# One kernel, several small reorderings: conversion steps at fixed places, operands at 128 bytes, a drain of GpSimd before the last expert

## The chip, the cores and the metric

The kernel runs on one core of a Trainium2 chip. The metric is the device time of one execution in microseconds (us). Three timed runs of the kernel before gave 777.03, 773.71 and 778.46 us; their median is 777.03. One further execution was recorded by the hardware profiler, and every row below comes from that one. The engines are TensorE (PE for its matmuls, PEld for the loads of stationary operands that run beside them), VectorE (DVE), ScalarE (ACT), GpSimd (POOL) and SyncE (SP, which only starts transfers).

## The reference, cut to what matters

Attention in chunks of 32 queries, each seeing 16 keys to the left, 8 to the right and 8 memory keys; a mixture of 8 experts in which each token has one expert and each expert exactly 384 tokens, given out greedily in the order of the gate's logits; and a last network with a SoLU (h times its softmax) and a normalisation.

```python
for c in range(nc):                                  # attention, per chunk of 32
    scores = scale * np.matmul(q_c, k_full.transpose(0, 1, 3, 2))
    a = np.exp(scores - max); a = a / (sum + 1e-09)
    out[:, :, c_start:c_end] = np.matmul(a, v_full)
logits = x @ w_gate                                  # x: 3072 x 512
for idx in np.argsort(-logits.flatten()):            # tok, e = idx // 8, idx % 8
    if assigned[tok] >= 0 or counts[e] >= cap: continue   # cap = 384
    assigned[tok] = e; counts[e] += 1
for e in range(8):                                   # w1: 512 x 1024, w2: 1024 x 512
    out[mask] = np.maximum(x[mask] @ w1[e], 0.0) @ w2[e]
h = x @ w_in                                         # 512 x 1024
solu = h * softmax(h)
ln = (solu - mean) / sqrt(var + 1e-06) * g_ln
return ln @ w_out                                    # 1024 x 512
```

## The kernel before, in words

**Attention** (`attention`, one loop of 29 turns over 24 tiles of 128 tokens, software-pipelined). For tile i: `score(i)` is 16 matmuls into a bank of scores and the row maxima `mx` on DVE; `less(i)` subtracts them (DVE, tile `p`); `expo(i)` is the exponential on ACT; `sums(i)` is the row sum `sum`, one small step on it, the reciprocal `rec` (all DVE) and the scaling of `p` by `rec` on GpSimd; `trans(i)` transposes p on PE into `t`, which ACT copies to `pt`; `pv(i)` multiplies with v into `o`; `xtrans` and `gate` make the logits `L`. One turn of the loop holds steps of five neighbouring tiles. The keys `kd`, queries `qt` and values `vd` come by transfers that SP starts some tiles ahead. At the end the attention output goes to memory as `x_dram`.

**Conversion.** The last network's two weight matrices arrive as eight-byte floats. `Fixed` turns chunks of 512 KB of them into pairs of single-precision operands (`in_h`, `in_l` and `out_h`, `out_l`): a transfer `raw`, one step on ACT, four on DVE (`e<-v`, `v<-v,e`, `e<-v`, `e<-raw,e`), and two on GpSimd (`v<-v,in_h`, `in_l<-v,e`). Up to seven chunks of w_in (CHUNKS_A) are worked on during attention.

**Routing** (`Route`). One round for each expert: a search of eight steps, each a chain of a few small PE and DVE instructions (`r<-oh,ge`, `sat`, `base`, `ge`), then the compaction that ends in the index list `idx` (`rhs`, `ohl`, `cc`, and `r<-cc,rep`, from which `idx` is made). A round also gives `iw`, the row list by which the expert's weights are fetched. Round 0 has nothing else to run beside it; the later ones run beside the expert before.

**Experts** (`Experts.run`). For expert r: GpSimd gathers three tiles `xg` of 128 rows of `x_dram` by `idx`; `x_prep` transposes each (PE, `tp`) and splits it into a high and a low half, `xh` (ACT) and `xl` (DVE). Each product of two fp32 matrices is three matmuls, high by high, high by low and low by high. `g12` computes h = x w1, hh and hl, and y += h w2, in nine turns f; `g3` computes the last network's h (three tiles t, 24 matmuls of 512 columns each) with `soft` behind it on ACT, DVE and GpSimd; `trans` and `g4` compute the output tile `o`, scaled on ACT into `ob`, which GpSimd scatters to `out` by `idx`. `first_w`, `split_w` make the weights' halves (`w1h` and `w2h` on ACT, `w1l` and `w2l` on DVE). Expert r's g4 runs one expert later, for the last expert at the very end.

**What sets the order.** The program is written out in order for each engine. `Pace` keeps a model clock for each engine; side work (conversion, routing, `soft`) stands in a list of generators, and each call of `beside` (that is `Pace.tick`) puts in the steps whose turn has come by these clocks. So where a side step lands among an engine's instructions is decided when the program is built. In attention the four DVE steps of a conversion chunk can land at any of the loop's `beside` calls. `route.stage` and `route.hold` say which routing round may run and when.

In the profile every instruction that goes through the clocks carries line 421; line 1295 is the start of the kernel and line 1303 its end. In the changed kernel these are lines 435, 1314 and 1322.

## Time and profile before, and how to read them

| what | before |
|---|---|
| timed runs, median (three runs) | 777.03 us (773.71 to 778.46) |
| the profiled execution, its own time | 779.07 us |
| the profiled execution, span of its instructions | 777.3 us |
| PE busy, of the span | 710.9 us, 91% |
| DVE busy, of the span | 518.1 us, 67% |
| chain that ended last, by engine | PE 54%, issue 17%, DVE 17%, DMA 5%, ACT 3%, POOL 2% |

The span is 1.8 us shorter than the execution's own time. Busy time of an engine is the time in which one of its instructions ran. The chain that ended last is followed back from the last instruction, at each step to whatever released it. The stages, by the clock of the trace: attention from 0 to 118.6 us, routing round 0 to 143.4, the first gather to 152.4, expert 0 (g12 and g3) to 221.1, experts 1 to 7 to 747, and the last three output tiles to 764.8; after that only the last scatter and the end of the program. A rate of the granted TensorE clock of 1.00 is 2.4 GHz, one of 0.50 is 1.2 GHz.

### The profile page before, as it was taken

The numbers are of one execution on the slowest core, as the hardware profiler recorded it, in microseconds if no ns is written. First come the engines' busy times: TensorE is split into PE (matmuls) and PEld (weight loads), VectorE is DVE, ScalarE is ACT, GpSimd is POOL, SyncE is SP. The second block draws the span as 40 slices with busy tenths as digits, with TensorE's granted clock in tenths as the row PEclk, the third lists the DMA queues.
The fourth block names the chain that finished last, engine by engine and source line by source line (L and its number), as shares of the span: only waits on it lengthen the run. The fifth ranks groups of instructions, "written<-read, shape, count | busy, mean of one in ns | idle before, by whom it ended". The sixth has DMA issues, their size and how long they took to land.

```text
span 777.3 us, 14615 instructions
## 1 busy us (share of the span) xinstructions
PE 710.9 (91%) x5771; PEld 613.4 (79%) x5771; DVE 518.1 (67%) x1398; ACT 341.6 (44%) x650; POOL 199.6 (26%) x263
## 2 busy tenths in 40 slices
PE   5888884589989999999999999999999999999993
PEld 3676664578879878988898889888988898899882
DVE  5788946578999977962996399549954842554150
ACT  4566640234384364423732463246324642563170
POOL 4354420532351162023202420232023201400121
PEclk9999995789999999999999999999999999999997
DMA  8999982441360062014201520151015200600100
GB/s 258 323 341 340 326 317 72 157 154 57 99 241 1 28 205 94 1 40 153 106 1 33 186 81 1 52 190 58 1 55 190 68 28 27 230 2 1 40 14 27
DMA packets 30020, 89.35 MB, mean 115 GB/s; under 512 B 4224, under 2 KB 4352, under 8 KB 29952
## 3 DMA queue, kind: packets, MB, share of 16 engines
q0 software_dynamic: 13056, 46.14, 17.4%
q1 hardware_dynamic: 16896, 42.28, 15.9%
q8 instruction: 45, 0.74, 0.4%
q14 instruction: 23, 0.19, 0.1%
HBM read 75.83 MB, written 12.58 MB: 114 GB/s over the span
## 4 chain that ended last, share of the span: by engine, by line
PE 54%; issue 17%; DVE 17%; DMA 5%; ACT 3%; POOL 2%; SPq 0%; POOLq 0%; DVEq 0%
PE h L421 24%; PE o L421 11%; PE y L421 10%; DVE e L421 4%; PE tp L421 3%; PE r L421 2%; DMA xg<-x_dram,idx 2%; DMA vd<-in_vx_dram 2%; DVE p L421 1%; DVE mx L421 1%; DVE v L421 1%; DVE ge L421 1%; DVE sum L421 1%; PE s L421 1%; PE xtp L421 1%
## 5 line engine op out<-in xcount | busy, mean ns | idle before, releaser
L421 PE MATMUL y<-hh,w2h 128*128 128x384 f32 x256 | 92.2, 360 | 4.8 <-DVE e L421 4.8
L421 PE MATMUL y<-hl,w2h 128*128 128x384 f32 x256 | 88.4, 345 | 2.0 <-DVE hl L421 2.0
L421 PE MATMUL y<-hh,w2l 128*128 128x384 f32 x256 | 87.4, 341 | 0.0
L421 POOL DMA_INDIRECT out_dram<-ob,idx x24 | 24.4, 1016 | 230.4 <-ACT ob L421 229.9
L421 POOL DMA_INDIRECT raw<-in_w_dram,iw x64 | 62.0, 968 | 81.6 <-PE r L421 34.8
L421 DVE TENSOR_REDUCE nm<-h 128x1 f32<-128x512 f32 x48 | 33.0, 688 | 70.7 <-PE h L421 70.4
L421 PE MATMUL o<-out_h,lh 128*128 128x512 f32 x192 | 77.4, 403 | 0.0
L421 PE MATMUL h<-in_h,yh 128*128 128x512 f32 x192 | 76.6, 399 | 0.0
L421 PE MATMUL h<-in_l,yh 128*128 128x512 f32 x192 | 76.0, 396 | 0.0
L421 PE MATMUL h<-in_h,yl 128*128 128x512 f32 x192 | 75.7, 394 | 0.0
L421 PE MATMUL o<-out_l,lh 128*128 128x512 f32 x192 | 75.4, 393 | 0.3 <-DVE out_l L421 0.3
L421 PE MATMUL o<-out_h,ll 128*128 128x512 f32 x192 | 75.1, 391 | 0.0
L421 ACT ACTIVATE hh<-h 128x384 fp32r<-128x384 f32 x64 | 31.4, 491 | 84.1 <-PE h L421 73.4
L421 ACT CAST w2h<-raw 128x512 fp32r<-128x512 f32 x64 | 39.4, 619 | 49.1 <-PE y L421 49.1
L421 PE MATMUL h<-xh,w1h 128*128 128x384 f32 x256 | 59.9, 347 | 0.4 <-ACT xh L421 0.4
L421 PE MATMUL h<-xh,w1l 128*128 128x384 f32 x256 | 58.4, 345 | 0.0
L421 PE MATMUL h<-xl,w1h 128*128 128x384 f32 x256 | 57.1, 344 | 1.1 <-DVE xl L421 1.1
L421 PEld LDWEIGHTS y<-hh,w2h 128*128 128x128 f32 x256 | 48.4, 189 | 7.5 <-DVE e L421 6.3
L421 DVE TENSOR_TENSOR xl<-tp,xh 128x512 fp32r<-128x512 f32 x24 | 16.6, 691 | 53.1 <-ACT xh L421 53.1
L421 ACT CAST w1h<-raw 128x512 fp32r<-128x512 f32 x64 | 39.6, 619 | 25.6 <-DVE idx L421 25.1
L421 PEld LDWEIGHTS y<-hl,w2h 128*128 128x128 f32 x256 | 48.6, 190 | 2.6 <-DVE hl L421 2.6
L421 DVE TENSOR_TENSOR w2l<-raw,w2h 128x512 fp32r<-128x512 f32 x64 | 43.7, 686 | 8.9 <-ACT w2h L421 8.9
(195 smaller groups left out, 1602.1 us busy)
## 6 DMA issues: line engine op xcount, KB each, us to landing
vd<-in_vx_dram SPq DMA_DIRECT2D x48, 256.0 KB, 5.7
kd<-in_kx_dram SPq DMA_DIRECT2D x48, 176.0 KB, 4.9
qt<-in_q_dram SPq DMA_DIRECT2D x24, 256.0 KB, 5.5
x_dram<-xs SPq DMA_DIRECT2D x6, 1024.0 KB, 9.7
raw<-in_win_dram SPq DMA_DIRECT2D x8, 512.0 KB, 6.0
raw<-in_wout_dram SPq DMA_DIRECT2D x8, 512.0 KB, 3.6
raw<-in_w_dram,iw POOLq DMA_INDIRECT x64, 5.7
xg<-x_dram,idx POOLq DMA_INDIRECT x24, 3.5
```

What stands on the lines that cost most here:

```text
L421: return fn(*args, **kw)
```

## The change

Seven edits. (1) The routing constants (`consts`) are made at the start, among the clearing of buffers, not spread over the first tiles. (2) The attention loop is put in another order: the sums of tile i-1 come first, then score and less of tile i, then up to about 0.65 us of conversion steps on DVE (`pace.fill("dve", ROOM)`, which goes over the 0.65 by the part of a step), the transposes of tile i-2, up to as much of conversion on ACT, the exponential of tile i, and then pv and xtrans of older tiles; `tick` no longer starts conversion steps on DVE in attention (`barred`). Chunks of w_in worked on in attention go from 7 to 6, and the first is fetched one tile sooner. The last group's gate products come in one piece. (3) A tile `pad` of 64 bytes per partition and a `spacer` of 128 bytes in place of 4 move the buffers behind them: the operands of the experts' matmuls then all start at multiples of 128 bytes in their partition. Before, `in_h`, `in_l` and `ident` do; `xh`, `xl`, `yh`, `yl`, `lh`, `ll`, `out_h` and `out_l` start 64 bytes past one, and `hh`, `hl`, the halves of w1 and w2, and `xg` 96 bytes past one. (4) Routing round 1 may start in the third turn of g12 of expert 0 (n = 4) and not ahead of it, and later rounds' stage is set at n = 2. (5) The dummy matmuls ahead of expert 0 write to another PSUM buffer. (6) The output tile of the very last g4 is scaled half on ACT and half on DVE; `soft` gives way once more ahead of its squaring step on ACT. (7) One `drain` of GpSimd stands behind the scatter of the last tile of expert 6, counted from 0.

```diff
@@ -36,12 +36,13 @@
 NEG = -1.0e30
 EVERY_OUT = 7.0
 SPARE_A = 1.38
-CHUNKS_A = 7
+CHUNKS_A = 6
 SIGNAL = 0.19
 EVERY_A = 8.8
 LATE = 1.5
-FIRST_A = 3
-FIRST_C = 8.0
+FIRST_A = 2
+PAD = 16
+ROOM = 0.65
 SPARE = 1.27
 FIT = 0.62
 FIT_OUT = 0.5
@@ -97,6 +98,8 @@
         clear(KD[1])
         nc.gpsimd.memset(KD[2], 0.0)
         nc.vector.memset(VD[0], 0.0)
+        for _ in consts():
+            pass
         clear(KD[3])
         nc.gpsimd.memset(VD[1], 0.0)
         clear(VD[2])
@@ -108,7 +111,6 @@
                 nc.sync.dma_start(wg, wgx)
             if i >= 4:
                 load_v(i - 4)
-        pace.add(consts(), FIRST_C, 0)
         P, PT, XT, mx = {}, {}, {}, {}
 
         def score(i):
@@ -219,21 +221,23 @@
         for i in range(NT + 5):
             if i == NT - 2:
                 pace.limit = 0
-            if i < NT:
-                s = score(i)
-                less(i, s)
-                load_kq(i + AHEAD)
             n = 0
             for _ in sums(i - 1) if 0 <= i - 1 < NT else ():
                 beside(i, n)
                 n += 1
-            if i >= NT and i - 2 < NT:
+            if i < NT:
+                s = score(i)
+                less(i, s)
+                pace.fill("dve", ROOM)
+                load_kq(i + AHEAD)
+            if 0 <= i - 2 < NT:
                 trans(i - 2)
+            if i < NT:
+                pace.fill("act", ROOM)
+                expo(i)
             beside(i, 3)
             if 0 <= i - 3 < NT:
                 pv(i - 3)
-            if i < NT:
-                expo(i)
             load_v(i + AHEAD - 4)
             if i == NT - 2:
                 for u in range(4):
@@ -246,15 +250,13 @@
                 xtrans(i - 4)
             if 5 <= i <= NT and (i - 5) % 4 == 3:
                 gate((i - 5) // 4)
-            if NT < i < NT + 4:
-                gate(NT // 4 - 1, (i - NT - 1,), 2)
+            if i == NT + 3:
+                gate(NT // 4 - 1, range(3), 2)
             if i == NT + 4:
+                gate_last(NT - 1)
                 gate_t(NT // 4 - 1, 3)
-                gate_last(NT - 1)
             if NT + 1 >= i >= 6 and (i - 6) % 4 == 3:
                 gate_t((i - 6) // 4)
-            if 2 <= i < NT:
-                trans(i - 2)
             beside(i, 4)
 
 
@@ -274,6 +276,7 @@
         self.tiles, self.rings = {}, {}
         self.jobs = []
         self.limit, self.spare, self.fit = 9, SPARE_A, FIT
+        self.barred = "dve"
         self.rush, self.late = RUSH, lambda: False
 
     def tile(self, ap):
@@ -388,12 +391,23 @@
             self.now += 0.1
         self.seen = self.now
         for job in list(self.jobs):
-            if job[2] <= self.limit and job[0] <= self.now and (
+            if job[2] <= self.limit and job[0] <= self.now and job[1] != self.barred and (
                     job[1] is None or self.clk[job[1]] <= (self.now + self.rush if self.late() else
                                                          min(self.now + self.spare, self.soon()))):
                 try:
                     self.until(job, next(job[3]))
                 except StopIteration:
+                    self.jobs.remove(job)
+
+    def fill(self, eng, room):
+
+        end = self.clk[eng] + room
+        for job in list(self.jobs):
+            while job[1] == eng and job[0] <= self.clk[eng] < end - 0.3 and job[2] <= self.limit:
+                try:
+                    self.until(job, next(job[3]))
+                except StopIteration:
+                    job[1] = None
                     self.jobs.remove(job)
 
     def soon(self):
@@ -552,7 +566,8 @@
         self.k = ctx.enter_context(tc.tile_pool(name="r_keep", bufs=1))
         self.w = ctx.enter_context(tc.tile_pool(name="r_work", bufs=1))
         self.idx, self.iw = {}, {}
-        self.held, self.stage, self.making, self.hold = False, 0, True, True
+        self.pad = self.k.tile([128, PAD], F32, name="pad")
+        self.held, self.stage, self.hold = False, 0, True
 
     def consts(self, ident):
 
@@ -608,7 +623,6 @@
             yield "spare", "dve"
             setattr(self, name, k.tile([128, n], F32, name=name))
             V.memset(getattr(self, name), value)
-        self.making = False
 
     def open_psum(self, ctx):
         self.ps = ctx.enter_context(self.tc.tile_pool(name="r_ps", bufs=1, space=PSUM))
@@ -870,7 +884,7 @@
         self.yl = k.tile([128, 4, CAP], F32R, name="yl")
         self.lh = k.tile([128, 8, CAP], F32R, name="lh")
         self.ll = k.tile([128, 8, CAP], F32R, name="ll")
-        self.spacer = k.tile([1, 1], F32, name="spacer")
+        self.spacer = k.tile([1, 32], F32, name="spacer")
         self.idx, self.iw = route.idx, route.iw
         self.W, self.C, self.Kc, self.XG, self.WS = {}, {}, {}, {}, {}
         self.scat = []
@@ -1068,6 +1082,7 @@
             self.done.add(("c", r, t, i))
         self.C[r, t] = e
         yield e
+        yield "spare", "act"
         junk = self.wk.tile([128, DM], F32, tag="ob", name="junk", bufs=2)
         A.activation(junk.bitcast(BF), e, AF.Square, accum_out=sq[:, t:t + 1])
         yield "act"
@@ -1127,14 +1142,19 @@
                 between()
         self.need("k", r, t)
         ob = self.wk.tile([128, DM], F32, tag="ob", name="ob", bufs=2)
-        nc.scalar.activation(ob, o, AF.Copy, scale=self.Kc[r][2][:, t:t + 1])
-        nc.gpsimd.memset(self.spacer, 0.0)
+        k, half = self.Kc[r][2][:, t:t + 1], DM // 2 if (r, t) == (E - 1, TT - 1) else DM
+        nc.scalar.activation(ob[:, 0:half], o[:, 0:half], AF.Copy, scale=k)
+        if half < DM:
+            nc.vector.tensor_scalar(ob[:, half:], o[:, half:], k, None, op0=ALU.mult)
+        nc.gpsimd.memset(self.spacer[:, 0:1], 0.0)
         st = nc.gpsimd.indirect_dma_start(
             out=self.out, out_offset=bass.IndirectOffsetOnAxis(ap=self.idx[r][:, t:t + 1], axis=0),
             in_=ob, in_offset=None)
         for o_ in self.scat:
             self.tc.declare_no_dep(st.ins, o_.ins, reason="every token has one row")
         self.scat.append(st)
+        if (r, t) == (E - 2, TT - 1):
+            self.tc.nc.gpsimd.drain()
 
     def run(self, steps):
 
@@ -1155,7 +1175,7 @@
         self.load_w(0, (1, 2))
         self.fixed.hold = False
         self.split_w(0, 0, (1,), True)
-        p = self.ph.tile([128, 4, 128], F32, tag="h", name="warm")
+        p = self.big.tile([128, 4, 128], F32, tag="big", name="warm")
         warm(nc, p, self.route.ones, 40)
         for t in range(TT):
             self.x_prep(0, t)
@@ -1165,7 +1185,6 @@
             self.split_w(0, f, (2,))
         for t in range(TT):
             self.need("x", 0, t)
-        self.route.hold = False
         self.beside.limit, self.beside.fit = 9, FIT_OUT
         self.beside.add(self.fixed.all(1, self.beside, EVERY_OUT, 0, 8))
         start = self.beside.now
@@ -1175,10 +1194,12 @@
             def extra(n, r=r):
                 if n == 2:
                     self.load_w(r, (3,))
+                    self.route.stage = r
+                if n == 4:
+                    self.route.hold = False
                 if r and n in TRANS_AT:
                     m = TRANS_AT.index(n)
                     self.trans(r - 1, m // 2, m % 2)
-            self.route.stage = r
             self.g12(r, extra)
             if r < 2:
                 self.need("y", r, 3)
@@ -1246,9 +1267,7 @@
         beside.tick()
 
     attention(nc, tc, q, kx, vx, wg, ident, x_dram, L, lambda: route.consts(ident), beside, step)
-    while route.making:
-        beside.tick()
-    beside.limit = 9
+    beside.limit, beside.barred = 9, ""
     route.open_psum(ctx)
     fixed.open_out(ctx)
     experts = Experts(ctx, nc, tc, x_dram, w1, w2, fixed, route, beside, ident, out)
```

On DVE in the attention loop, one chunk's first two conversion steps (`e<-v`, `v<-v,e`) stand before like this, between the sums of one tile and the maximum `mx` of the next:

```order
L421 TENSOR_REDUCE mx<-s 128x8
L421 TENSOR_TENSOR p<-s,mx 128x4x2x64
L421 TENSOR_REDUCE sum<-p 128x8
L421 TENSOR_SCALAR sum<-sum 128x8
L421 RECIPROCAL rec<-sum 128x8
L421 TENSOR_SCALAR e<-v 128x512
L421 TENSOR_SCALAR L<-g 128x32
L421 SCALAR_TENSOR_TENSOR v<-v,e 128x512
L421 MEMSET s 32x8x16
L421 TENSOR_REDUCE mx<-s 128x8
L421 TENSOR_TENSOR p<-s,mx 128x4x2x64
```

and in the changed kernel like this:

```order
L435 TENSOR_REDUCE mx<-s 128x8
L435 TENSOR_TENSOR p<-s,mx 128x4x2x64
L435 TENSOR_SCALAR e<-v 128x512
L435 SCALAR_TENSOR_TENSOR v<-v,e 128x512
L435 TENSOR_SCALAR L<-g 128x32
L435 TENSOR_REDUCE sum<-p 128x8
L435 TENSOR_SCALAR sum<-sum 128x8
L435 RECIPROCAL rec<-sum 128x8
L435 MEMSET s 32x8x16
L435 TENSOR_REDUCE mx<-s 128x8
L435 TENSOR_TENSOR p<-s,mx 128x4x2x64
```

The two steps have moved from behind the row sums, where the next tile's `mx` was queued behind them, to behind the subtraction `p<-s,mx`, where the same tile's row sums are queued behind them.

On PE, where expert 0's g3 (`h<-in_h,yh` and its two companions, 72 matmuls) ends and expert 1's g12 (`h<-xh,w1h`) begins, the three transposes of the gathered rows (`tp<-ident,xg`) stand apart among the matmuls of g3 before. The first of the three stands so (39 of the 72 are ahead of it, and `r<-cc,rep`, the last product of the routing round, is behind the 12th):

```order
L421 MATMUL h_3278<-in_l,yh 128x512
L421 MATMUL h_3278<-in_h,yl 128x512
L421 MATMUL tp<-ident,xg 128x128 x4
L421 MATMUL h_3278<-in_h,yh 128x512
L421 MATMUL h_3278<-in_l,yh 128x512
L421 MATMUL h_3278<-in_h,yl 128x512
```

and in the changed kernel all three stand together behind the 72nd, with `r<-cc,rep` behind the 59th:

```order
L435 MATMUL h_3277<-in_h,yh 128x512
L435 MATMUL h_3277<-in_l,yh 128x512
L435 MATMUL h_3277<-in_h,yl 128x512
L435 MATMUL tp<-ident,xg 128x128 x12
L435 MATMUL h<-xh,w1h 128x384 x4
L435 MATMUL h<-xh,w1l 128x384 x4
```

So 13 matmuls of g3 stand between the last product of the routing round and the first transpose, where 27 stood before, and no matmul is left beside the second and the third.

On DVE, between the copy `cc` that this product reads and the index list `idx` made from it, the changed kernel has three steps of the next expert's weights:

```order
L435 CAST cc<-r 128x12
L435 TENSOR_TENSOR w2l<-raw_3203,w2h 128x512
L435 TENSOR_TENSOR w1l<-raw_3201,w1h 128x512
L435 TENSOR_TENSOR w2l<-raw_3203,w2h 128x512
L435 TENSOR_SCALAR idx_3350<-r 128x3
```

Before, one conversion step `e<-v`, one `e<-raw,e` and one row maximum `nm` stand between the two. The drain has no place in this list, which shows no sequencer instructions; on GpSimd it is followed by the small steps `na`, `nv` of the last expert's `soft`.

## Rows read from the trace of the kernel before

**Rows 1.** Windows: stretch, length, busy PE PEld DVE ACT POOL, PEclk, DMA share, GB/s.
```profile
60.00:80.00 20.00, 16.75 (x396) 13.21 (x392) 17.73 (x37) 12.98 (x25) 9.61 (x9) 1.00 0.96 338
152.40:221.10 68.70, 65.43 (x508) 55.50 (x509) 60.00 (x150) 30.91 (x59) 26.55 (x23) 0.95 0.42 137
300.00:400.00 100.00, 98.86 (x588) 88.22 (x587) 73.39 (x221) 42.73 (x82) 18.86 (x27) 1.00 0.21 72
```

**Rows 2.** Timeline, DVE in attention: start, duration, instruction, [idle before it <-its releaser].
```profile
61.51 0.69 DVE L421 TENSOR_REDUCE mx<-s 128x8 f32<-128x512 f32 x1
...
64.00 0.68 DVE L421 TENSOR_REDUCE mx<-s 128x8 f32<-128x512 f32 x1
...
67.85 0.69 DVE L421 TENSOR_REDUCE mx<-s 128x8 f32<-128x512 f32 x1 [1.11 <-PE s L421]
...
70.30 0.38 DVE L421 TENSOR_SCALAR e<-v 128x512 int32<-128x512 int32 x1
70.71 1.43 DVE L421 SCALAR_TENSOR_TENSOR v<-v,e 128x512 int32<-128x512 int32 x1
...
73.25 0.68 DVE L421 TENSOR_REDUCE mx<-s 128x8 f32<-128x512 f32 x1
```

**Rows 3.** Tiles mx and v on DVE: count, ns min/median/max, first to last start.
```profile
L421 DVE TENSOR_REDUCE mx<-s x10: 640/684/692, 61.5 to 97.4; 128x8 f32<-128x512 f32 x10
...
L421 DVE SCALAR_TENSOR_TENSOR v<-v,e x6: 1411/1423/1434, 34.3 to 92.4; 128x512 int32<-128x512 int32 x6
```

**Rows 4.** Timeline: GpSimd beside a conversion step, and such a step later on.
```profile
70.55 1.04 POOL L421 TENSOR_TENSOR p<-p,rec 128x512 f32<-128x512 f32 x1 [1.70 <-DVE rec L421]
...
203.93 0.68 DVE L421 SCALAR_TENSOR_TENSOR v<-v,e 128x512 int32<-128x512 int32 x1
```

**Rows 5.** Timeline, PE from the first gather into g12 of expert 0.
```profile
151.09 0.66 PE L421 MATMUL tp<-ident,xg 128*128 128x128 f32 x4 [1.12 <-DVE xl L421]
...
152.42 0.97 PE L421 MATMUL h<-xh,w1h 128*128 128x384 f32 x4 [0.40 <-ACT xh L421]
...
158.46 0.44 PE L421 MATMUL y<-hl,w2h 128*128 128x384 f32 x1 [1.43 <-DVE hl L421]
...
174.73 0.16 PE L421 MATMUL r<-some,ones 15*128 15x1 f16 x1 [0.78 <-DVE sat L421]
```

**Rows 6.** Windows of PE alone: stretch, length, busy, PEclk, DMA share, GB/s.
```profile
161.00:167.80 6.80, 6.80 (x49) 0.50 0.31 93
```

**Rows 7.** Timeline, GpSimd's first gather for expert 0.
```profile
143.85 1.40 POOL L421 DMA_INDIRECT xg<-x_dram,idx  x1 [4.18 <-ACT w1h L421]
```

**Rows 8.** Timeline, the second gather: DVE, GpSimd and PE.
```profile
207.29 0.15 DVE L421 TENSOR_SCALAR idx<-r 128x3 int32<-128x3 f32 x1
...
207.71 1.07 POOL L421 DMA_INDIRECT xg<-x_dram,idx  x1 [1.95 <-DVE el L421]
...
212.03 0.66 PE L421 MATMUL tp<-ident,xg 128*128 128x128 f32 x4 [0.33 <-DMA xg<-x_dram,idx]
...
223.74 0.44 PE L421 MATMUL h<-xl,w1h 128*128 128x384 f32 x1 [1.08 <-DVE xl L421]
```

**Rows 9.** Groups by form, PE: count, ns min/median/max, first to last start.
```profile
L421 PE MATMUL o<-out_h,lh x24: 389/389/481, 642.6 to 659.3; 128*128 128x512 f32 x24
...
L421 PE MATMUL h<-in_h,yh x24: 394/394/394, 659.9 to 676.0; 128*128 128x512 f32 x24
```

**Rows 10.** Timeline of GpSimd, and the sequencer instructions of the last line.
```profile
730.36 0.96 POOL L421 DMA_INDIRECT out_dram<-ob,idx  x1 [4.42 <-ACT ob L421]
737.39 0.19 POOL L421 TENSOR_TENSOR na<-s 128x1 f32<-128x1 f32 x1 [6.08 <-ACT e L421]
...
766.32 0.96 POOL L421 DMA_INDIRECT out_dram<-ob,idx  x1 [4.32 <-ACT ob L421]
...
L1303 SPq EVENT_SEMAPHORE  x11: 17/28/28, 769.1 to 777.2; - x11
L1303 POOLq DRAIN  x3: 45/102/10418, 766.1 to 777.0; - x3
```

## The prediction, made before the changed kernel ran

> **What bounds the kernel now.** I read the stretches of the span first, since an average over the span hides that its stages have different limits. From 300 to 400 us PE is busy 98.86 of 100 us at full clock [rows 1], and the table puts it at 91% of the whole span: experts 1 to 7 are a stream of matmuls with no room, and nothing in the change takes matmuls out of it. What a reordering can win lies outside: in attention, in the first two handoffs and g12 of expert 0 (65.43 busy of 68.70 us, clock 0.95), and behind the last matmul.
>
> In attention no engine is full, but three are near it. From 60 to 80 us the DMA engines are busy 0.96 of the time at 338 GB/s, DVE 17.73 and PE 16.75 of 20 us [rows 1]. DVE's timeline shows its turn: from one `mx` to the next 2.49 us without conversion (61.51 to 64.00), and 5.40 us with four conversion steps in between, which fill 70.30 to 73.25 [rows 2]. Over ten starts, 61.5 to 97.4, the turn is 35.9/9 = 3.99 us [rows 3].
>
> **The change, part by part**, against the profiled execution's own 779.07 us.
>
> *Attention.* Before, the next tile's `mx` waits behind the conversion steps, and behind `mx` the whole tile. After, they stand behind `p<-s,mx`, where DVE would wait for the exponential before it can sum. So a turn without conversion is two steps of 0.69, the wait, and the sums; the wait is hidden under a pair of steps when there is one. The second point is `v<-v,e`: six times in attention it took 1411 to 1434 ns [rows 3], beside GpSimd's `p<-p,rec` (70.55, 1.04 us, against 70.71), while the same step took 0.68 us at 203.93 with GpSimd just before its own step [rows 4]. In the new order `mx` and `p<-s,mx`, 1.4 us, stand between `rec` and the conversion, so GpSimd has done with `p`. Six times 0.73 us is 4.4 us. DVE alone would give more: at 3.5 us a turn (2.49 plus some 1.0 for the exposed wait or a pair of steps) the 15 turns from 37 to 97 us would save 7. But transfers are busy 0.96 of that time: at 338 GB/s the stage's loads can give back little more than the 4% in which they idle, 2.4 us in 60, and one chunk less (0.52 MB, 1.6 us at that rate). Both together are 4.0, about what the pairing alone gives. I take **-4.5**, bounds 0 (transfers set it anyhow) and -8 (DVE's own sum). The constants go under the first loads, and cost nothing; without that cover they'd be some 3 us.
>
> The Trainium skill ("SBUF — State Buffer", "SBUF: two separate sides") says that a VectorE instruction with two SBUF inputs and a GpSimd one that reads SBUF take one pair of ports in turn, the loser blocked for the whole instruction. The 1.43 against 0.68 us agree. By it alone, GpSimd's conversion steps (1.28 us) can still hold one up in the new order, and the gain would be nearer 2 us.
>
> *First handoff.* The third transpose waits 1.12 us for `xl` of the first tile [rows 5], because it shares a buffer with the dummy matmuls. With these elsewhere it waits for its gather alone. I take **-0.7**, bounds 0 and -1.1.
>
> *g12 of expert 0.* PE waits 1.43 us for `hl` at 158.46, as DVE works off the routing search first, and 0.78 for `sat` [rows 5]; soon after, from 161.0 to 167.8, it runs at half clock with no idle time [rows 6], which costs 3.4 us. The search now starts in the third turn of g12. The wait for `hl` goes, and I think the slow stretch with it, as it came right behind those waits; waits of the search's own kind come back. I take **-4.8** (1.43 + 3.4), bounds -1.4 and -5.6.
>
> *Second handoff.* The price of that. The last routing product now has only 13 matmuls of g3 behind it, at 16.1/23/3 = 0.233 us each [rows 9], 3.0 us. Then come three weight steps ahead of `idx` on DVE (at 0.6 us, about the 0.68 of the step of this size [rows 4], some 2.0 us with `idx`), 0.42 us to the first gather (207.29 to 207.71 [rows 8]), and from there to the first matmul of g12 what the first handoff took, 143.85 to 152.42, less the 1.12 that is not needed [rows 5, 7], 7.45. That is 9.9, less the 3.0 and an estimated 1.3 for the transposes themselves (0.66 for four [rows 8], overlapping): PE idles 5.6 us. Before, it idled 0.33 and 1.08 [rows 8]. The loss is 4.2. Behind such a gap a stretch at half clock is likely; rows 6 price a long one at 3.4, I take 1.0. Together **+5.2**, bounds +2.7 (the weight steps done early) and +7.6. The same order holds for later experts as before, and nothing is added there.
>
> *Alignment.* Matmuls on in_h, which lies on a 128-byte border already, take 394 ns; those on out_h, 64 bytes off one, 389 [rows 9]. So the traces give no sign that a border helps. I take 0, bounds 0 and -2.9 (576 matmuls of g3 by 5 ns).
>
> *Tail.* Half of the last `ob` on each engine: **-0.3**.
>
> *The drain.* GpSimd's last drain took 10.418 us, from 766.1, so to 776.5, though SP, waiting for the last scatter's data, was released at 769.1; two other drains took 0.045 and 0.102 us [rows 10]. So 7.4 us lie behind all data. Either it is work put off for each of the 112 indirect transfers (64 weights, 24 gathers, 24 scatters), 66 ns each, or a fixed delay after any. If the first, the new drain does it for 109 of them and the last one keeps 3: -7.2. The new one stands behind the scatter of 730.36; GpSimd's next work starts at 737.39 [rows 10], and the first scatter behind it is over 20 us off, so even 10 us there are hidden; without that cover they'd be 3 us on the last `soft`. If the second, 0. Nothing in the trace has a drain in mid-kernel. A drain with little to do is short, and a delay that outlasts the data by 7.4 us looks more like a list being worked off than like one transfer: I take **-7.2**, by a little.
>
> Sum: -4.5 - 0.7 - 4.8 + 5.2 - 0.3 - 7.2 = -12.3 us, that is 766.8 for the profiled execution. The median of the timed runs is 2.0 lower, 777.03, and so the forecast is **764.7**; without the drain, 771.9.
>
> **Rivals.** *The drain's delay is fixed* (against: the 0.045 and 0.102 us; for: both come right behind another drain, so they say little): 771.9.
>
> *Transfers set attention, and the second handoff takes all it can*: 0 for attention, +7.6 for the handoff. With the drain's gain 771.6, without 778.8.
>
> *Slower: the exponential comes late.* ACT's conversion steps now stand ahead of the tile's exponential, and DVE's sums wait for it. If ACT had 0.65 us of them in front of every exponential, with what it copies for other tiles (ACT is busy 12.98 of 20 us [rows 1]), a turn would be 1.4 + 1.6 + 1.1 on DVE plus a step, 4.5 us. Twenty-four turns by 0.5 over the present 3.99 are +12 and the 4.5 are not won: 788.4 without the drain's gain, 781.2 with it. It decides from a turn of 4.2 us on. Against it: only 12 of 24 turns have such a step.
>
> *Matmuls gain from the border.* The Trainium skill ("TensorE: Matmul & The Clock Gate", "Back-to-back issue gap") gives 216 ns as a gap for 512 columns, 17 under the 0.233 here; it doesn't name the address. As a mechanism in rows: if the 20 ns over 512/2.4 GHz that g3 shows were due to the address, and as much as 14 in the other 2112 matmuls of 384 and 512 columns, up to 40 us would go; a third of it gives 751. Against: 394 on the border, 389 off it.
>
> **How the numbers follow.** The drain's gain with the other terms near their values 0.42: 764.7, own range 758 to 770. Fixed delay with the others near theirs 0.34: 771.9, 766 to 779. Exponential late, or all of the second rival without the drain's gain, 0.14: 779 to 788. Border 0.10: 740 to 757. One per cent, about what measurement can tell from no change, is 7.8 us: faster means under 769.3. That is 0.40 of the first case, 0.07 of the second and 0.10 of the last: 0.57. Slower, over 784.8, is the greater part of the late exponential without the drain's gain: 0.09. The rest, 0.34, is within 1%. The range from 755 to 781 leaves out most of the border and the upper half of the slow case, 0.18.
>
> **What would show it.** The last drain on line 1322: under 1 us if put-off work, near 10 if fixed; a second row of some 7 to 10 us near 720. In attention `v<-v,e` at 0.7 us and a `mx` turn of 3.6 to 3.8; a turn over 4.2 with DVE idle for `p<-ACT` is the slow rival. No half clock in expert 0's g12; 5 to 6 us of PE waiting for `xg` and `xh` at the start of expert 1. The matmul of g3 at 394 ns again. The prediction is wrong if the drain's 10.4 us stay, or if the second handoff costs over 10 us.

## The result, and the profile after

Four runs of the changed kernel gave 764.3 to 765.93 us, median 765.27; four of the kernel before 773.71 to 778.46, median 776.16. The ratio is 0.9845, with a 95% interval of 0.981 to 0.988: the changed kernel is faster by 1.2 to 1.9%. The forecast was 764.7 (755 to 781). The medians differ by 10.9 us. The profiled execution took 764.67 us, its span is 762.9, 14.4 less than before; that is more than 10.9, since the profiled execution of the kernel before was 2.9 us above its median. The forecast sum, -12.3, lies between the two; its terms came out otherwise, as the next rows show. They cut the span into four stages: up to the first matmul of g12 of expert 0, from there to that of expert 2, then to the last matmul, and the end.

The windows of the changed kernel (from:to, length, busy us of PE, PEld, DVE, ACT and POOL, granted clock, DMA share, GB/s):

```profile
0.00:138.80 138.80, 105.72 (x2231) 83.39 (x2231) 102.17 (x267) 65.93 (x120) 52.02 (x58) 0.90 0.81 286
138.80:298.40 159.60, 145.72 (x943) 124.65 (x944) 135.13 (x343) 76.09 (x144) 53.61 (x57) 0.95 0.33 110
298.40:756.80 458.40, 458.40 (x2598) 405.58 (x2597) 285.41 (x789) 198.42 (x386) 93.29 (x147) 1.00 0.20 70
756.80:762.90 6.10, 0.43 (x2) 0.01 (x1) 0.48 (x1) 0.47 (x1) 0.96 (x1) 0.93 0.11 43
```

The same four windows of the kernel before:

```profile
0.00:152.40 152.40, 109.14 (x2231) 88.35 (x2231) 107.45 (x273) 68.13 (x122) 54.86 (x61) 0.88 0.77 265
152.40:300.00 147.60, 141.72 (x942) 120.58 (x943) 128.18 (x342) 74.14 (x142) 50.66 (x55) 0.98 0.34 114
300.00:764.80 464.80, 459.71 (x2599) 404.50 (x2597) 282.45 (x785) 198.68 (x386) 93.13 (x147) 1.00 0.20 69
764.80:777.30 12.50, 0.39 (x2) 0.00 (x0) 0.00 (x0) 0.69 (x1) 0.96 (x1) 0.65 0.06 21
```

| stage | before | changed | difference | forecast |
|---|---|---|---|---|
| attention, routing round 0, first gather | 152.4 | 138.8 | -13.6 | -5.2 |
| experts 0 and 1 | 147.6 | 159.6 | +12.0 | +0.4 |
| experts 2 to 7 | 464.8 | 458.4 | -6.4 | 0 |
| behind the last matmul | 12.5 | 6.1 | -6.4 | -7.5 |

So two gains were missed (8.4 and 6.4 us) and one loss was (11.6), and they nearly cancel. PE's busy time is what it was (710.3 for 710.9); all that moved is waiting. In experts 2 to 7 PE now never stands still.

**Attention.** DVE's timeline answers to [rows 2]: a pair of conversion steps stands behind `p<-s,mx`, and from one `mx` to the next there are 3.46 us (5.40 for four steps before, 2.49 for none):

```profile
62.64 0.64 DVE L435 TENSOR_REDUCE mx<-s 128x8 f32<-128x512 f32 x1
63.39 0.69 DVE L435 TENSOR_TENSOR p<-s,mx 128x512 f32<-128x512 f32 x1
63.99 0.42 DVE L435 TENSOR_SCALAR e<-v 128x512 int32<-128x512 int32 x1
64.45 0.69 DVE L435 SCALAR_TENSOR_TENSOR v<-v,e 128x512 int32<-128x512 int32 x1
65.06 0.68 DVE L435 TENSOR_REDUCE sum<-p 128x8 f32<-128x512 f32 x1
...
66.10 0.69 DVE L435 TENSOR_REDUCE mx<-s 128x8 f32<-128x512 f32 x1
```

The groups of tile v (count, ns min/median/max, first to last start), answering to [rows 3], and the window from 60 to 80 us, answering to [rows 1]:

```profile
L435 DVE SCALAR_TENSOR_TENSOR v<-v,e x5: 693/693/693, 41.5 to 87.0; 128x512 int32<-128x512 int32 x5
```

```profile
60.00:80.00 20.00, 19.82 (x454) 15.25 (x449) 17.33 (x37) 13.49 (x26) 10.69 (x10) 1.00 0.99 351
```

The step takes 693 ns where it took 1411 to 1434, transfers run at 0.99 and 351 GB/s for 0.96 and 338, and PE is busy 19.82 of 20 us for 16.75.

**Experts 0 and 1.** PE's timeline at the second gather, answering to [rows 8], and in the first g4, where a wait stands that the kernel before does not have:

```profile
209.86 0.66 PE L435 MATMUL tp<-ident,xg 128*128 128x128 f32 x4 [1.59 <-DMA xg<-x_dram,idx]
211.17 0.66 PE L435 MATMUL tp<-ident,xg 128*128 128x128 f32 x4 [0.64 <-DMA xg<-x_dram,idx]
212.60 1.12 PE L435 MATMUL tp<-ident,xg 128*128 128x128 f32 x4 [0.78 <-DMA xg<-x_dram,idx]
214.39 1.01 PE L435 MATMUL h<-xh,w1h 128*128 128x384 f32 x2 [0.67 <-ACT xh L435]
...
282.68 0.80 PE L435 MATMUL o<-out_h,lh 128*128 128x512 f32 x1 [2.90 <-ACT out_h L435]
```

Four waits in a row, 3.7 us, and matmuls behind both places at half clock: the first `tp` took 0.66 us for four and the third 1.12, the first `o` 0.80 where [rows 9] has 0.39 (the granted clock is 0.66 in the mean over 210:220 us, and over 280:290 too).

**The end.** The drains of GpSimd, by line: 1157 is the new one, 1322 the end of the program (count, ns min/median/max, first to last start); then SP's release by the last scatter's data, and the two halves of the last output tile:

```profile
L1157 POOLq DRAIN  x1: 10168/10168/10168, 722.1 to 722.1; - x1
...
L1322 POOLq DRAIN  x3: 51/102/3117, 758.4 to 762.5; - x3
...
L1322 SPq EVENT_SEMAPHORE  x11: 17/28/28, 761.4 to 762.8; - x11
```

```profile
757.40 0.47 ACT L435 ACTIVATE ob<-o,k 128x256 f32<-128x256 f32 x1 [4.80 <-PE o L435]
...
757.91 0.48 DVE L435 TENSOR_SCALAR ob<-o,k 128x256 f32<-128x256 f32 x1 [8.91 <-ACT ob L435]
```

The last drain is 3.1 us long for 10.4 [rows 10], and ends at 758.4 + 3.1 = 761.5, right behind the landing at 761.4. The new one is 10.2 us long, from 722.1 to 732.3, and GpSimd's next step starts at 732.4, 10.0 us behind the scatter where it was 7.0 [rows 10]: the drain held it for some 3 us, and nobody waited.

### The profile page after: what moved, and what is told of

Read it like the earlier page. It is cut to its first block, busy times and chain, and to the rows that moved or that the text cites. A ratio compares the mean times of both kernels' runs of the same rounds, so it can differ in the third digit from the quotient of the medians.

```text
span 762.9 us, 14656 instructions
## 1 busy us (share of the span) xinstructions
PE 710.3 (93%) x5771; PEld 613.6 (80%) x5771; DVE 523.2 (69%) x1399; ACT 340.9 (45%) x650; POOL 199.9 (26%) x263
## 4 chain that ended last, share of the span: by engine, by line
PE 74%; DVE 16%; issue 4%; DMA 2%; ACT 2%; POOL 1%; SPq 0%; POOLq 0%; DVEq 0%
PE h L435 30%; PE o L435 17%; PE y L435 16%; PE tp L435 4%; PE r L435 3%; DVE e L435 3%; PE s L435 1%; PE xtp L435 1%; DVE ge L435 1%; DVE sum L435 1%; PE t L435 1%; DVE p L435 1%; DMA xg<-x_dram,idx 1%; DVE nm L435 1%; DVE v L435 1%
## 5 line engine op out<-in xcount | busy, mean ns | idle before, releaser
L435 ACT ACTIVATE ob<-o,k 128x512 f32<-128x512 f32 (+1 forms) x24 | 16.3, 679 | 81.6 <-PE o L435 79.3
L435 DVE SCALAR_TENSOR_TENSOR hl<-h,hh 128x384 fp32r<-128x384 f32 x64 | 35.4, 553 | 21.6 <-ACT hh L435 21.4
L435 PEld LDWEIGHTS y<-hl,w2h 128*128 128x128 f32 x256 | 48.9, 191 | 1.2 <-DVE hl L435 1.2
```

What stands on the lines that cost most here:

```text
L435: return fn(*args, **kw)
```

## The experiments

Twelve kernels were run in three groups, e1 to e4, e5 to e8 and e9 to e12, each group on one chip, together with the kernel before. That kernel took 780.3, 775.4 and 783.6 us (median) on the three chips. Where the chip matters, stages of the profiles are compared; each stage below is that of one profiled execution. "A" to "D" below are the four stages of the table above.

| run | time, ratio to before (95%) | A | B: experts 0, 1 | C: 2 to 7 | D: end |
|---|---|---|---|---|---|
| before | 776.2 | 152.4 | 147.6 | 464.8 | 12.5 |
| changed | 765.3, 0.9845 (0.981 to 0.988) | 138.8 | 159.6 | 458.4 | 6.1 |
| e5, changed again | 765.4, 0.9873 (0.983 to 0.992) | 139.8 | 158.4 | 458.4 | 6.1 |
| e1, no drain | 779.1, 0.9985 (0.996 to 1.001) | 143.2 | 160.0 | 458.8 | 12.9 |
| e6, before and the drain | 769.4, 0.9926 (0.989 to 0.996) | 150.3 | 146.0 | 464.6 | 5.7 |
| e12, drain at expert 3 | 779.6, one run | 149.5 | 159.6 | 461.5 | 7.2 |
| e8, conversion ahead of mx | 774.1, 0.9971 (0.995 to 0.999) | 148.1 | 159.5 | 458.4 | 6.2 |
| e4, seven chunks | 772.0, 0.9896 (0.986 to 0.993) | 143.3 | 160.5 | 458.9 | 6.1 |
| e7, no pad | 763.7, 0.9834 (0.980 to 0.987) | 141.9 | 158.6 | 457.5 | 6.1 |
| e3, no new point in soft | 772.7, 0.9893 (0.985 to 0.993) | 144.7 | 160.9 | 458.9 | 6.0 |
| e11, stage at the start | 773.7, 0.987 (0.982 to 0.992) | 144.6 | 155.5 | 465.8 | 6.0 |
| e2, round 1 at the start | 762.6, 0.9775 (0.974 to 0.981) | 144.8 | 151.0 | 458.9 | 6.0 |
| e9, the same, last tile on ACT | 764.8, 0.9751 (0.972 to 0.979) | 147.0 | 152.4 | 458.9 | 5.7 |
| e10, round 1 at n = 2 | 766.5, 0.9779 (0.974 to 0.982) | 145.6 | 155.0 | 458.9 | 5.7 |

**The base again (e5).** No edit.

> The changed kernel itself once more, on the chip of this call, as the base for the three others and for the four runs before, in which PE waited some 4.8 us for xh in the first gather where the changed kernel's profile showed under 0.5. If that wait belongs to the chip and not to the edits, it stands here too, and the time is 4 to 5 us over 765.3 with the kernel before some 4 us over its 776; if it came with the edits, the time is 765.3 again.

It took 765.44 us, on a chip where the kernel before took 775.4. Its stages are those of the first profile within 1.2 us, and PE waits only 0.4 us for `xh` there. So the longer first stage of e1 to e4 and e9 to e12, of which 4.8 to 5.7 us are a wait of PE for `xh` in the first gather, came with their chips (the kernel before is slower there too), not with edits: e1 and e12 have the instructions of the changed kernel, in its order, up to the drain.

**The drain (e1, e6, e12).** In e1 it is taken out, in e6 it is the only edit on the kernel before, in e12 it stands elsewhere. The edit of e12:

```diff
-        if (r, t) == (E - 2, TT - 1):
+        if (r, t) == (3, TT - 1):
             self.tc.nc.gpsimd.drain()
```

> The changed kernel without the drain behind expert 6's last scatter; all else as changed. Put-off work (my theory, one share for each indirect transfer): the last drain is near 10.4 us again, of which 7 to 7.5 behind the landing of the last data, and the time is about 772.5 us, 7.2 over the changed kernel. Rival, that the drain's delay is fixed and the shorter tail comes from the output tile halved between ACT and DVE: the last drain stays at 3.1 us and the time at 765.3.

> The kernel before with the one drain behind expert 6's last scatter added, nothing else. Put-off work: the last drain falls from 10.4 to some 3 us, none of it behind the landing of the data, and the time by 6.5 to 7.5. Fixed delay, or a drain in mid-kernel that holds up the last expert: 0, or some us more.

> The changed kernel with the drain behind the last scatter of expert 3 and not of expert 6. Put-off work, one share of some 66 ns for each transfer since the last drain: some 52 of 112 transfers are left for the last drain (4 experts' scatters, gathers and weights, part of them issued earlier), so it ends about 3.5 us behind the landing of the data and takes 6.5 to 7 us, and the one in the middle takes 4 to 5 us less than 10. Rival, one fixed price that the first drain of the kernel pays: the last drain stays at 3.1 us and the middle one at about 10.

The sequencer's drains of e1, of e6 (line 1139 is the new one) and of e12 (line 1157), in this order, columns as above:

```profile
L1320 POOLq DRAIN  x3: 45/102/10417, 763.7 to 774.6; - x3
```

```profile
L1139 POOLq DRAIN  x1: 10173/10173/10173, 726.2 to 726.2; - x1
...
L1305 POOLq DRAIN  x3: 51/102/3116, 762.2 to 766.3; - x3
```

```profile
L1157 POOLq DRAIN  x1: 7005/7005/7005, 517.1 to 517.1; - x1
...
L1322 POOLq DRAIN  x3: 51/102/4702, 772.2 to 777.4; - x3
```

Without the drain the end is 12.9 us again, 6.9 more; alone on the kernel before it brings 12.5 down to 5.7, and the time by 0.4 to 1.1%. e12 rules out a fixed price. From the last indirect transfer's end on GpSimd to the drain's end there are 9.22 us with 112 transfers since the last drain (before), 8.97 with 109 (the new drain), 5.79 with 70 and 3.50 with 42 (the two of e12): 82 ns for each, from any two of these, and next to nothing besides. Other counts fit worse: the time since the last drain gives 11 to 14 ns per us, the number of all GpSimd instructions 34 to 39 ns each. Every one of these transfers moves 128 rows, so a price per transfer and one per row can't be told apart here. With 3 it is 1.92, which is the landing of the data. So e12's last drain was expected at 6.5 to 7 us and took 4.7, as the work runs beside the landing and is not added to it (42 times 82 ns are 3.4 us). e12's time is a single run and is not compared; but its stage C is 2.6 us longer than that of e9 and e10 on its chip. GpSimd's next weight transfer starts 6.6 us behind the end of expert 3's last scatter, 0.3 without a drain there, and at 540 us PE waits 1.6 us for `hh` and 0.6 for `hl`, which it does not in e9. So a drain with transfers queued close behind it is not free; how it makes these waits was not followed.

**The place of the conversion steps (e8).**

```diff
             if i < NT:
+                pace.fill("dve", ROOM)
                 s = score(i)
                 less(i, s)
-                pace.fill("dve", ROOM)
```

> The changed kernel with the conversion steps of attention one place earlier: in front of the tile's mx, behind the sums of the tile before, where they mostly stood before the change; in the same amounts. Theory: they then run beside GpSimd's scaling of p (v<-v,e back at 1.4 us) and every step holds up the next tile: a turn with a pair of steps gets 1.5 to 2 us longer, and the last scores start 5 to 9 us later than in the changed kernel. Rival: transfers set the pace of attention now, so it is 0 to 2 us later.

DVE's timeline of e8 and its group of `v<-v,e`:

```profile
66.73 0.20 DVE L435 RECIPROCAL rec<-sum 128x8 f32<-128x8 f32 x1
66.85 0.38 DVE L435 TENSOR_SCALAR e<-v 128x512 int32<-128x512 int32 x1
67.26 1.43 DVE L435 SCALAR_TENSOR_TENSOR v<-v,e 128x512 int32<-128x512 int32 x1
68.62 0.68 DVE L435 TENSOR_REDUCE mx<-s 128x8 f32<-128x512 f32 x1
69.40 0.69 DVE L435 TENSOR_TENSOR p<-s,mx 128x512 f32<-128x512 f32 x1
70.79 0.69 DVE L435 TENSOR_REDUCE sum<-p 128x8 f32<-128x512 f32 x1 [0.69 <-ACT p L435]
```

```profile
L435 DVE SCALAR_TENSOR_TENSOR v<-v,e x5: 1431/1434/1435, 40.3 to 95.2; 128x512 int32<-128x512 int32 x5
```

One line moved one place earlier costs 774.12 against 765.44 us on the same chip, 8.7 us. The two-input step is back at 1.43 us in the five recorded cases, and DVE then sits idle for 0.69 behind `p<-s,mx`, for the exponential, which the pair had covered. The last matmul of the scores starts at 102.8 us, 8.6 later than in e5 (94.2). The kernel before has it at 102.2 in its own profile, and on the chip of e5 and e8 at 100.3 (e6, whose attention is that kernel's). So the place of these steps is worth more than the whole gain up to the last scores on this chip, 6.0 us: in the old place the rest of the new order is 2.5 us slower than the kernel before (one profile each). How much of the 8.6 is the longer step (five times 0.74 us) and how much the next tile held up, no run separates.

**The count of chunks (e4).** `CHUNKS_A = 7` in place of 6.

> The changed kernel with 7 chunks of w_in in attention as before, not 6. Theory: the chunk left over pushes the conversion of w_out back, so that the first g4 waits 2.9 us for out_h and runs on at half clock (about 2 us); with 7 chunks this wait goes and the time falls by 3 to 5, to 760 to 762. Rival, that attention is bound by transfers and DVE: the chunk costs there what it wins later (1.5 us of transfer and 2 us of DVE steps), and the time stays within 1.5 us of 765.3.

The edit did not do what it says: in e4 the seventh transfer of w_in starts at 117.1 us, as in e1, behind attention, since at the fixed places no more than six chunks get through. The stages of e4 are those of e1 within 0.6 us, and PE still waits 2.6 us for `out_h`. All engines have the instructions of the changed kernel in the same order, so e4 is the changed kernel once more, on this chip, and its ratio of 0.9896 is what the change brings there: 8.3 us. What a seventh chunk would do is left open. That 772.0 lies 7.1 under e1, on the same chip, is the drain.

**The addresses (e7).** The pad is taken out, and the spacer is 4 bytes again.

> The changed kernel with the pad taken out and the spacer of 4 bytes again, so that the operands lie where they lay before, 64 and 96 bytes past a border of 128. Theory: the address does nothing; matmuls of g3 start every 0.233 us and those of g4 every 0.227 as in both kernels, and the time is that of the changed kernel on this chip within 1.5 us. Rival: the border is worth 5 ns or more in some of the 2688 matmuls, 3 us or more slower without it.

763.73 us, 1.7 below e5, with intervals that overlap: the border gains nothing here. If anything it costs: stage C is 457.5 us in e7 and 458.4 in both e5 and e8 on the same chip. Groups by form in the changed kernel, answering to [rows 9], have the matmul of g3 at the same duration as before (busy us, mean ns of one | idle before it):

```profile
L435 PE MATMUL h<-in_h,yh 128*128 128x512 f32 x24 | 9.5, 395 | 0.0
```

**Who freed y (e3, e11).** In experts 3 to 6 of the kernel before the first matmuls of g12 into y waited four times for the step `e` of the last `soft`; DVE had the next round's first search step ahead of it, and ACT the squaring of the tile before ahead of its exponential. The change touches both. e3 takes out the new point in `soft`; e11 sets `route.stage` at the start again:

```diff
-        yield "spare", "act"
```

```diff
                 if n == 2:
                     self.load_w(r, (3,))
-                    self.route.stage = r
...
+            self.route.stage = r
             self.g12(r, extra)
```

> The changed kernel without the new point in soft that lets other ACT work go ahead of the squaring step. In the kernel before, y of experts 3 to 6 waited 4.8 us in four waits for the step e of the last soft, whose exponential stood behind the squaring step of the tile before; these waits are gone in the changed kernel. Theory: the new point removed them, so they come back: 4 to 6 us more, about 770. Rival, that the later start of the routing rounds' steps on DVE (stage set at n = 2) removed them: no change, 765.3.

> The changed kernel with the stage of the later routing rounds set at the start of each expert's g12, as before, and not in its second turn; release of round 1 as changed. Theory, after e3: the later stage keeps the first search step of the next round off DVE while it still owes the last soft its step e, and that removed the waits of y. So they come back in experts 3 to 6, and experts 2 to 7 take 4.5 to 6.6 us longer: 770 to 772. Rival, that the new point in soft does it after all, or the two only together: no more than 1.5 us.

Waits of PE in the kernel before and in e11 from 300 us to its end (what waited for what: us, times, longest):

```profile
PE y L421 <- DVE e L421: 4.8, 4, 1.3
...
PE y L435 <- DVE e L435: 4.7, 4, 1.3
```

e3 contradicts the theory it was run for: experts 2 to 7 take 458.9 us without the new point too. e11 has them at 465.8 and the four waits back. So the later stage alone won these 6.4 us. The four waits account for 4.7 or 4.8 of them; the rest was not followed further. The gain has a price, which e11 shows too: its stage B is 155.5 us, where e12, with the later stage on the same chip, has 159.6. The wait for `out_h` in the first g4 is gone in e11, although the late release of round 1 is still there: from expert 1's g3 to expert 2's g12 it takes 38.0 us, for 42.7 in e12. So the later stage and the late release make this wait together, and beside the late release the later stage wins only some 3 us net (6.9 in C against e9, less 4.1 in B).

**The release of round 1 (e2, e9, e10).** In e2 the hold ends ahead of g12 of expert 0, as before the change; e9 is the same with the last tile scaled on ACT alone; e10 ends it at n = 2, also with ACT alone:

```diff
         for t in range(TT):
             self.need("x", 0, t)
+        self.route.hold = False
...
-                if n == 4:
-                    self.route.hold = False
```

> The changed kernel with routing round 1 released ahead of expert 0's g12 as in the kernel before (the later stage of the other rounds is kept). Theory: the late release costs PE about 6 us at the start of expert 1 (waits for the gathered rows, then a stretch at half clock) and wins nothing lasting in g12 of expert 0; so the second handoff goes back to about 1 us of waiting and the time falls by 3 to 6, to 759 to 762. Rival, that the late release pays in g12 of expert 0: the wait for hl and a half-clock stretch come back there, some 5 us, and the time stays within 1.5 us of 765.3.

> The changed kernel with routing round 1 released ahead of expert 0's g12 (as in e2) and the last output tile scaled on ACT alone. On a chip without the long wait for xh in the first gather: second handoff back to about 1 us of waiting (-6), no 2.9 us wait for out_h in the first g4 and no slow stretch behind it (-5), a wait for hl or sat of 1 to 3 us in g12 of expert 0, and the last scatter 0.3 us sooner behind the last matmul. Together 6 to 9 us under the changed kernel, 757 to 760. Rival, that e2's gain was made by its chip: within 2 us of the changed kernel's 765.

> As e9, but with the round released one turn into g12 of expert 0 (n = 2), halfway between the kernel before and the changed one. If the second handoff decides, the index list comes with 40 of 72 matmuls of g3 still to run, enough for the gather: as good as e9 or 1 us better, as the wait for hl at the start of g12 is out of the way. If the wait for out_h hangs on the release as well, it may stand here in part: 2 to 4 us over e9.

PE's timeline of e2 at the second gather:

```profile
204.86 0.60 PE L435 MATMUL tp<-ident,xg 128*128 128x128 f32 x4
208.09 0.60 PE L435 MATMUL tp<-ident,xg 128*128 128x128 f32 x4
212.02 0.60 PE L435 MATMUL tp<-ident,xg 128*128 128x128 f32 x4
216.50 1.65 PE L435 MATMUL h<-xh,w1h 128*128 128x384 f32 x4 [3.88 <-ACT xh L435]
```

The transposes stand among the matmuls of g3 again and wait for nothing. Experts 0 and 1 take 151.0 us for 158.4 (e5) to 160.5 (e4, on the chip of e2). The parts of that: g12 of expert 0 takes 48.9 us in e2, 49.4 in e5 and 49.3 before, so the late release wins nothing there; from the first matmul of g3 to expert 1's g12 it is 22.9, 25.9 and 19.4; from expert 1's g3 to expert 2's g12, with the first g4 in it, 36.8, 42.4 and 37.0. The `out_h` wait is gone in e2, which keeps the later stage. Its second handoff still has a wait of 3.88 us for `xh`, which on this chip stands at the first handoff too. In time, e2 took 762.6 us where e4, in effect the changed kernel, took 772.0 on the same chip: the late release, beside the later stage, costs 9.4 us there. e9 came out at 0.9751 of the kernel before, under the changed kernel's interval, the best ratio here; the changed kernel with its drain in place was not timed on that chip, so the 0.9% between them are a comparison across chips, but its stage B is there in e12: 159.6 us for 152.4. e10 lies between (155.0), against the hope that it would be as good.

The last scatter starts 1.53 us behind the start of the last matmul with ACT alone (e6, e9, e10, and before) and 1.83 with the tile halved (changed, e1 to e5, e7, e11, e12; 2.11 in e8).

## Why the prediction came out right, and which of its steps did not

The time came out near the forecast in good part by luck: by stages the terms are off by -8.4, +11.6, -6.4 and +1.1 us, which add up to -2.1. What was right for its reason are the drain, the first handoff, the alignment and the mechanism in attention.

**Attention, -4.5: mis-sized, -13.6 with the handoff (-10.5 on one chip, e6 to e5).** The mechanism stood as told: pairs hidden behind the exponential, `v<-v,e` at 0.69 us. The Trainium skill ("SBUF — State Buffer", "SBUF: two separate sides") on two-input steps beside GpSimd agrees with 1.43 us in e8 and 0.69 in the changed kernel; by it the gain was put lower still, as GpSimd's own conversion steps might hold others up, and in attention that did not show on DVE. The GpSimd steps themselves got longer: `v<-v,in_h` takes 1.72 to 1.73 us in four of five cases, 1.28 in five of six before. The step of the prediction that failed is the cap. I took the transfers' idle share from 60 to 80 us alone, 4%, for the whole stage. From 20 to 100 us they idle more. The kernel before, the changed kernel, and on one chip e6 (the attention of the kernel before) and e5:

```profile
20.00:100.00 80.00, 65.92 (x1497) 53.13 (x1487) 68.42 (x145) 48.10 (x92) 34.29 (x35) 0.95 0.92 322
...
20.00:100.00 80.00, 74.11 (x1662) 57.10 (x1654) 63.06 (x136) 51.68 (x100) 32.67 (x28) 1.00 0.98 351
...
20.00:100.00 80.00, 66.91 (x1528) 53.79 (x1531) 68.83 (x144) 49.93 (x95) 36.02 (x37) 0.97 0.93 327
...
20.00:100.00 80.00, 72.12 (x1633) 55.76 (x1626) 62.92 (x136) 51.81 (x98) 32.71 (x28) 1.00 0.96 338
```

That is 9% more bytes in 80 us between the first two, 7 us by itself, and 3%, some 3 us, on the one chip. The loop had held the transfers up as well as they held the loop: e8, with the steps one place earlier, has them at 0.91 and 315 GB/s on the chip of e5. DVE's own sum, which I set aside as the bound, gave 7 to 8. Up to the last scores the gain is 10.0 us between the first two profiles and 6.0 between e6 and e5, for 4.5 forecast. One profile alone is uncertain by some us here: e12, with the same instructions, reaches the last scores at 99.0 us, and e5 at 94.2. Between the last scores and the routing's first product another 2.8 us went (18.2 to 15.4; 3.8 between e6 and e5), which no run took apart.

The constants, taken at nothing, do show: they hold DVE until 10.2 us, and the first `mx` starts at 10.40 us where it started at 8.60. Whether these 1.8 us last to the end of attention no run shows.

**First handoff, -0.7: right.** From the first routing product to g12, 32.1 us became 31.2, and the wait for `xl` is gone.

**g12 of expert 0, -4.8: wrong, +0.9.** The wait for `hl` went from 1.43 to 0.94, but a new one of 3.26 came at 156.3, for the search's first `ge`:

```profile
144.57 0.44 PE L435 MATMUL y<-hl,w2h 128*128 128x384 f32 x1 [0.94 <-DVE hl L435]
...
156.32 0.75 PE L435 MATMUL r<-oh,ge 128*15 128x8 bf16 x24 [3.26 <-DVE ge L435]
```

and some half clock behind it (means of 0.90 over 150:160 and 0.93 over 160:170, which make some 3.4 us of it, half of what [rows 6] has). DVE comes late to it, as GpSimd conversion steps, of the chunks that are left over from attention, run beside its own steps, which then take longer. GpSimd and DVE ahead of that place, twice:

```profile
144.42 1.30 POOL L435 TENSOR_TENSOR v<-v,in_h 128x512 f32<-128x512 f32 x1
...
152.85 1.49 POOL L435 TENSOR_TENSOR in_l<-v,e 128x512 fp32r<-128x512 f32 x1
```

```profile
144.43 1.85 DVE L435 TENSOR_TENSOR w1l<-raw,w1h 128x512 fp32r<-128x512 f32 x1
...
153.25 1.31 DVE L435 TENSOR_TENSOR L<-L,el 128x192 f32<-128x192 f32 x1
```

The first step takes 0.68 us when alone (at 139.41). The second belongs to the search itself and takes 0.35 or 0.36 in the six later rounds; so does `gone`, 1.28 us at 151.52 for 0.17. These two make 2.1 of the 3.26 us. That I took "waits of the search's own kind come back" for small was the fault. That the left-over chunks are the cause was argued, not shown: e4, which was to test it, did not move them.

**Second handoff, +5.2: right, +6.0.** e2 shows that the late release makes it. The parts were sized otherwise: PE waits 3.7 us and not 5.6, and the half clock, for which I took 1.0, fills some 6.8 of the 10 us from 210 to 220 (a mean of 0.66).

**Missed: the first g4, +5.7.** "The same order holds for later experts as before" was read from the order of PE alone. There the order is the same, but ACT's cast of `out_h` is late, at 281.91 behind the squaring step of `soft`, PE waits 2.9 us, and half clock follows. It goes with round 1 released early (e2), and also with the stage set at the start (e11): it takes both edits.

**Missed: experts 2 to 7, -6.4.** I priced the later `stage` at nothing, though PE is busy 459.7 of 464.8 us there before. PE at 98.9% in [rows 1] was read as "no room"; 1.1 us in 100 over 465 us are 5 us, four waits of one cause, and e11 names it.

**The drain, -7.2, taken "by a little": right, -6.9.** The price is 82 ns for each transfer, not 66, and overlaps the landing; that is why the last drain took 3.1 us and not, as I had put it, under 1: it starts ahead of the last scatter and lasts until its data have landed. **The halved tile, -0.3: wrong sign, +0.3.** DVE's half starts at 757.91, when ACT's is done at 757.87: the two halves of one tile run one behind the other. **Alignment, 0: right.** (e7)

The exponential was never late: from 37 to 95 us DVE waited 0.69 to 0.87 us for it in five turns without conversion and not at all behind a pair. The mean turn over all 24 tiles is 3.6 us (`mx` from 10.40 to 93.65), 4.1 before (8.60 to 102.84). The longest from 37 us on, 4.7, holds a wait of 0.63 us for PE's scores.

## What to carry to other kernels

A step on an in-order engine belongs where that engine would wait anyhow: the same two conversion steps cost 8.7 us of 765 one place earlier, since there they hold up the next tile and run beside GpSimd's reads. When a chain is released later so that it doesn't disturb the work beside it, count what its last link has left to hide under, and whatever else is ordered behind it on the other engines. If the program ends with a long drain of GpSimd, count the indirect transfers since the last one and drain in the shadow of other work, where no transfer of GpSimd is queued close behind; and look at 1% of waiting in a long steady stage before calling it full.

## What the runs showed that was not expected

A drain of GpSimd costs 82 ns for each indirect transfer since the last drain (9.22, 8.97, 5.79 and 3.50 us for 112, 109, 70 and 42), and the work can be done in parts. On two chips PE waited 4.8 to 5.7 us for `xh` in the first gather in all eight profiles; in the two first profiles and the four of e5 to e8 it waited 0.4, with either kernel. Up to three of ACT's casts there start 1.6 to 5.9 us behind transposes that are recorded as done, and what holds them is open. Two halves of one output tile written by ACT and DVE ran one after the other, 0.47 and 0.48 us, slower than 0.69 on ACT alone.
